# Summing the two halves of eight converted weights on TensorE instead of VectorE, with a scheduler that counts no handover within an engine

## The chip, the cores and the metric

The kernel runs on one core of a Trainium2 chip. The core has a matrix engine (TensorE, PE in the profile; PEld is its loading of weights), a vector engine (VectorE, DVE), a scalar engine (ScalarE, ACT), a general engine (GpSimd, POOL) and SyncE (SP), which here issues the DMA transfers. Each engine works through its own queue in order; semaphores order work between engines. SBUF is the working memory of 128 partitions, PSUM holds eight banks of 128 x 512 float32 that TensorE writes. The metric is the device time of one execution in microseconds, as a median of repeated runs.

## What is computed

The reference has two parts. The first is a normalised linear attention over 8 batches, 8 heads, 576 positions and a head size of 64:

```python
kv = np.einsum('bhsd,bhse->bhde', k, v)
out = np.einsum('bhsd,bhde->bhse', q, kv)
rms = np.sqrt(np.mean(out * out, axis=-1, keepdims=True) + 1e-06)
x = (out / rms * g_norm)            # then (B,H,S,D) -> (B*S, H*D): 4608 x 512
```

The second is an MLP with softplus, with w_in of 512 x 2048 and w_out of 2048 x 512:

```python
h = x @ w_in
g = np.maximum(h, 0.0) + np.log1p(np.exp(-np.abs(h)))
return (g @ w_out).astype(np.float32)
```

q, k, v and g_norm are float32, the two weight matrices float64. The kernel gets each float64 element as two 32-bit words and has to turn them into float32 itself.

## The kernel before

**Matrix products.** The large products use the F32R type of TensorE[...]. So every operand is split into three F32R parts (a high part, a remainder scaled up by 4096, and a correction), and each product is made of three passes summed in one PSUM bank.

**Stages.** Tokens are taken in 36 tiles of 128. `kv_of` (line 647) loads k and v of one batch and makes kv (matmuls of line 676, plain F32). `rows` (line 687) makes one tile of x: q is transposed (line 756 by TensorE for the first two batches, line 731 by VectorE later), multiplied by kv (line 700), squared and reduced (773, 704), its root taken on POOL (707, 708), scaled (712) and, for the first tiles, transposed by TensorE (718), split (620, 623, 626) and stored (782, 783). In a first phase, `step` (line 829) walks over blocks of 384 tokens and chunks of 128 hidden units, four chunks for the first four blocks and six for the others: `mm1` (line 843, 12 matmuls) into one of two PSUM banks of the ring "h", softplus and splitting on ScalarE and VectorE (865, 867, 854, 858), then `mm2` (line 850, 9 matmuls per step) into three banks of sums. Two later phases do the remaining hidden units in blocks of 512 tokens with fewer products by a form of fast matrix multiplication (`wide_step`, line 1008; matmuls of lines 1030 and 1100).

**Weights.** The two matrices are cut into 16 chunks each, so 32 weights of 128 x 512; weight j = 2c is chunk c of w_in and j = 2c+1 chunk c of w_out. `weight` (line 394) fetches one (512 KB, line 403) and converts it: ScalarE makes a mask (`square`, 414), VectorE makes from the high word a float32 t with the upper bits (`high1` 418, `high2` 422, `mask` 427), then its power of two p (`power`, 435), then the low word's share on the scale of p, in place (`rest`, 440), and at last `total` (444) adds t and p into w. ScalarE's `beyond` (431) records numbers out of range. `split_weight` (line 471) then makes the three parts: `high` (481 or 483, ScalarE), `low` (488 or 491, VectorE), `low_up` (494, ScalarE); for the first eight weights (c < 4) the third difference is made by TensorE in a bank of ring "h" (`less_by_pe`, 505 and 506) and read by ScalarE (509); for the others by VectorE and ScalarE (497, 501).

**What sets the order.** The order of instructions on every engine is fixed when the kernel is built, by the planner `Plan` (line 54). Each piece of work is a task with an engine, a planned duration, the tasks it comes after, a position `pos` (lower goes first among tasks that can start within 150 ns of each other) and the buffers it takes and gives back. Buffers come from rings: "m" is eight SBUF places of 128 x 512, "h" the two PSUM banks. A task's planned end is its start and duration plus the handover of its engine (line 61: 250 ns for PE, 120 for ACT and DVE, 150 for POOL, 0 for SP); a task becomes ready at the latest end of those before it (line 194). Where the planner sees a hole of 400 ns or more on PE in the opening, it puts in a dummy matmul (`warm`, line 1181), which needs a bank of ring "h" too. The lists P0 to P7 (lines 249 to 257) hold the positions: P0 those of converting and fetching the first eight weights and offsets between stages, P1 to P3 those of later weights and of the wide phases, P4 those of the 36 tiles, P5 those of kv and q, P6 those of the wide operands, P7 those of the first loads of k, v and q.

Of the kernel before, what the change touches and what calls it, by code (L numbers as in the profile page):

```python
# [8 lines left out]
F32 = mybir.dt.float32  # L9
# [9 lines left out]
P = 128  # L19
# [36 lines left out]
class Plan:  # L56
# [19 lines left out]
    def slot(self, ring):  # L76
        return Slot(ring)

    def add(self, engine, ns, run, after=(), pos=0.0, take=(), give=(), size=0, behind=None, follows=None, kind="all"):
        t = Task(engine, ns, run, [a for a in after if a is not None], pos, list(take), list(give), size)  # L80
        for s in t.give:
            s.readers += 1
        self.tasks.append(t)
        t.follows = follows
        t.behind = behind
        t.kind = kind
        return t

    def order(self):
# [5 lines left out]
        ready = {}  # L95
# [28 lines left out]
        while left:  # L124
            best = None
            for engine, tasks in ready.items():
                options = []
                for t in tasks:
                    at = max(engine_free[engine], t.ready)
                    if t.size:  # L130
                        at = max(at, dma_free - 2500)
                    for i, s in enumerate(t.take):
                        others = sum(u.ring == s.ring for u in t.take[:i])
                        if engine == "SP" and s.ring in ("m", "n"):
                            others += self.KEEP
                        if len(free[s.ring]) <= others:
                            break
                        at = max(at, sorted(free[s.ring])[sum(u.ring == s.ring for u in t.take[:i])][0])
                    else:
                        options.append((at, t))  # L140
                if not options:
                    continue
                first = min(at for at, _ in options)
                options = [(at, t) for at, t in options if at <= first + self.SOON]
                small = [o for o in options if engine == "PE" and o[1].kind != "all"]
                if small:
                    rest = [o for o in options if o[1].kind == "all"]
                    if kind != "all":
                        options = [o for o in small if o[1].kind == kind] or small
                    elif rest and len(small) < self.TOGETHER and (  # L150
                            min(o[1].pos for o in small) + self.PATIENCE > min(o[1].pos for o in rest)):
                        options = rest
                at, t = min(options, key=lambda o: (o[1].pos, o[0]))
                if engine == "PE" and self.spare and self.spare[-1].start is None:
                    ring, run, ns, _ = self.spare
                    begin = max(engine_free["PE"], self.BEGIN, min(free[ring])[0] if free[ring] else at)
                    if begin + ns <= at:
                        s = Slot(ring)
                        at, t = begin, Task("PE", ns, lambda s=s: run(s), [], None, [s], [s], 0)
                        t.kind = "all"  # L160
                        s.readers = 1
                if best is None or at < best[0]:
                    best = (at, t)
            if best is None:
                raise RuntimeError("the plan is stuck at " + str([(e, t.pos, [s.ring for s in t.take if not free[s.ring]]) for e, ts in ready.items() for t in ts][:20]))
            at, t = best
            if t in ready[t.engine]:
                ready[t.engine].remove(t)
                left -= 1
            for s in t.take:  # L170
                place = min(free[s.ring])
                free[s.ring].remove(place)
                s.place = place[1]
                if t.pos is not None:
                    coming[s.ring] = coming.get(s.ring, 0) - 1
            if t.engine == "PE":
                t.ns += self.SWITCH.get((kind, t.kind), 0)
                kind = t.kind
            t.start = at
            engine_free[t.engine] = at + t.ns  # L180
            t.end = at + t.ns + self.HANDOVER[t.engine]
            if t.size:
                dma_free = max(dma_free, at + t.ns) + t.size
                t.end = dma_free + (self.LANDING if dma_free > self.FILLED else 2000)
            for s in t.give:
                s.readers -= 1
                last_read[id(s)] = max(last_read.get(id(s), 0), t.end)
                if not s.readers:
                    free[s.ring].append((last_read[id(s)], s.place))
                    retire(s.ring)  # L190
            for u in users.get(id(t), ()):
                waiting[id(u)] -= 1
                if not waiting[id(u)]:
                    u.ready = max([a.end for a in u.after] + ([u.follows.start] if u.follows else []), default=0)
                    ready.setdefault(u.engine, []).append(u)
            done.append(t)
        return sorted(done, key=lambda t: t.start)
# [3 lines left out]
def kernel(  # L201
# [24 lines left out]
    nc = tc.nc  # L226
    B, H, S, D = q.shape
    d_model, d_ff = moe_w_in.shape
# [17 lines left out]
    STEPS = [(ph, n, p) for ph in (1, 2) for n in range(n_wide) for p in PAIRS[ph - 1][n]]  # L246
    LAST = 2

    P0 = [-45.94, -26.77, -11.8, 0.28, -29.91, -5.64, -2.86, 3.84, -103.4, -98.98, -69.3, -76.66, -68.5, -24.67, -23.22, -34.97, 8.15, -43.02, 7.47, 9.69, 7.18, 18.16, -12.1, 4.75, 1.0, 95.98, -6.45, 6.38, 7.69, 5.17]
    P4 = [-30.17, -6.08, 16.93, -33.9, -22.35, -28.91, -17.33, -7.12, -9.75, -2.59, 0.87, 2.93, -12.14, -3.26, 0.98, 3.76, 7.8, -3.0, -2.25, 7.68, 20.89, 50.27, -0.5, -0.13, 26.66, 22.67, -11.61, -5.55, 2.74, 0.64, -0.48, 1.34, 0.64, 1.68, -8.4, -1.37]  # L250
    P5 = [1.24, -5.69, -2.28, 1.58, 5.58, 0.43, 5.83, -7.56, 3.01, -2.95, 3.18, 1.42, -14.52, 0.57, -1.29, -1.34]
    P6 = [-0.39, 4.6, -0.28, -2.24, -0.01, 1.05, 1.77, -3.9, -2.15, 0.85, 1.85, -1.74, 6.34, -2.44, -0.13, 3.82, 7.89, 0.51]
    P7 = [-23.78, -17.98, -11.85, -14.93, 0.41, 1.61, 7.35, 2.7, -25.02, -6.6, -15.2, -4.48, -2.14, 0.64, 2.93, 0.97, 4.67, 5.36, 3.33, 6.57, -10.37, 2.36, -14.11, -9.89, -7.11, 12.91, -2.89, 14.55, 12.59, 9.35]
    CONVERT, FETCH, EARLY, LATER = P0[:8], P0[8:16], P0[16:27], P0[27:]
    P1 = [48.8, 48.65, 66.31, 74.64, 125.35, 131.27, -11.31, 54.26, 67.75, 469.13, 282.82, 195.86]
    P2 = [22.14, 35.93, 25.02, 37.31, 52.38, 81.67, 74.61, 116.65, 106.27, 111.35, 100.82, -152.23, 99.52, 221.41, 428.54, -173.95, 119.58, -155.43, 317.87, 212.07, -7.69]
    P3 = [3.0, 2.86, 5.84, -16.31, 1.53, 3.03, 3.55, -20.64, 3.15, 2.55, 1.38, 1.52, 1.27, 0.75, 2.42, -1.39]
    SPLIT = {p: (P1[i], P1[6 + i]) for i, p in enumerate((2, 3, 4, 5, 6, 7))}
    TAKEN = {c: (P2[c - 6], P2[4 + c]) for c in range(6, 16)}
    LEAD, APART, AHEAD, MM2, LATE, SPLIT_G = P3[0], P3[1], P3[2], P3[3:11], P3[11:14], P3[14]  # L260
# [13 lines left out]
    ident = ident_r.bitcast(F32)  # L274
# [10 lines left out]
    def space(name, words, late, dtype=F32):  # L285

        if (name, late) not in spaces:
# [13 lines left out]
                 h=2, o=2, tp=1, s0=1, s1=1, s2=1, s3=1, w=15, wh=3, u=4, u1=1, gvp=2, xl=2, ab=2)  # L301
# [9 lines left out]
    slot, add = plan.slot, plan.add  # L311
# [67 lines left out]
    wide = moe_w_in.dtype != F32  # L379
# [14 lines left out]
    def weight(j, pos, fetch_pos, behind):  # L394

        c, of_out = divmod(j, 2)
        raw, w = slot("rawb" if j % 2 and c < 8 else "raw"), slot("m")
        words = 2 if wide else 1

        def fetch():  # L400
# [6 lines left out]
        if wide:  # L407
            sq, t, p = (slot(n) for n in ("sq", "m", "m"))
# [40 lines left out]
            d2 = add("DVE", 690, high2, [d1], pos, [], [raw])  # L449
            d3 = add("DVE", 690, mask, [d2, a1], pos, [])  # L450
            over_done.append(add("ACT", 910, beyond, [d3], pos + (4 if c < 4 else 0), [], [sq]))
            d4 = add("DVE", 430, power, [d3], pos, [p, w])
            d5 = add("DVE", 690, rest, [d4], pos, [], [raw])
            ready = add("DVE", 690, total, [d3, d5], pos, [], [t, p])
        else:
            ready = add("DVE", 450, lambda: nc.vector.tensor_copy(new(w, [P, d_model]), raw.tile[:, :, 0]),
                        [f], pos, [w], [raw])
# [130 lines left out]
    def load_q(b):  # L588


        q_slots[b], q_loads[b] = slot("qa"), []
        pos = x_pos(first_tile[b] + 1) - EARLY[7] + P5[B + b]

# [555 lines left out]
    for c in range(KF):  # L1149
        for j in (2 * c, 2 * c + 1):  # L1150
            if c < OWN:
                pos = CONVERT[j] if c < 4 else LATER[c - 4] + LATER[2] * (j % 2)
                weight(j, pos, FETCH[j] if c < 4 else pos, pos - 3.5)
            else:
                fetch, pos = (x + P2[20] * (j % 2) for x in TAKEN[c])
# [61 lines left out]
```

## Time and profile before

The median of three runs is 872.99 us (872.97 to 874.07). The profiled execution took 873.68 us, and its span, from the first to the last instruction, is 871.7 us.

| engine | busy us | share of the span | instructions |
|---|---|---|---|
| PE | 858.2 | 98% | 6464 |
| PEld | 761.2 | 87% | 6464 |
| DVE | 703.9 | 81% | 992 |
| ACT | 521.4 | 60% | 979 |
| POOL | 78.3 | 9% | 79 |

Busy time is the union of an engine's instructions; an instruction's length runs from its start to its written end, and neighbours on one engine can overlap, so the step from one start to the next can be shorter than a length. The chain that ended last is followed back from the last instruction to what released it, step by step; what is not on it had slack. The granted TensorE clock is given as a share of full speed.

### The profile page before, as it was taken

What the parts mean: (1) busy time and instruction counts of PE and PEld (TensorE: products, weight loads), DVE (VectorE), ACT (ScalarE), POOL (GpSimd) and SP (SyncE); (2) the same over time, 40 slices, a digit from 0 to 9 for tenths busy, and PEclk for the clock granted to TensorE, in tenths of its full rate; (3) what the DMA queues carried; (4) which work ended last, traced back from release to release, by engine and by line L of the source; (5) the groups of instructions that cost most, each with busy time, mean ns of one, the idle gap of its engine ahead of it and who ended that gap; (6) DMA issues with size and microseconds to landing.
All of it is one profiled execution on the core that took longest, in us unless ns stands there. A gap on an engine that the chain in (4) does not pass through costs nothing.

```text
span 871.7 us, 17016 instructions
## 1 busy us (share of the span) xinstructions
PE 858.2 (98%) x6464; PEld 761.2 (87%) x6464; DVE 703.9 (81%) x992; ACT 521.4 (60%) x979; POOL 78.3 (9%) x79
## 2 busy tenths in 40 slices
PE   7899999999999999999999999999999999999998
PEld 5678888989898899988998988888899899999996
DVE  7888898988788788798988789877788766878873
ACT  5776564445353567766657556654877555566653
POOL 0351234121112300000000000000000000000000
PEclk9899999999999999999999999999999999999999
DMA  9999999898993765427544546656364653777764
GB/s 270 275 231 206 283 243 253 152 267 210 221 175 102 178 194 170 156 85 243 183 156 147 182 157 192 196 158 180 110 195 136 237 162 107 243 225 234 236 189 129
DMA packets 239634, 167.07 MB, mean 192 GB/s; under 512 B 106304, under 2 KB 198464, under 8 KB 239552
## 3 DMA queue, kind: packets, MB, share of 16 engines
q1 hardware_dynamic: 239392, 165.99, 68.2%
q8 instruction: 50, 0.82, 0.4%
q14 instruction: 32, 0.26, 0.1%
q10 hardware_dynamic: 160, 0.00, 0.0%
HBM read 112.98 MB, written 52.95 MB: 190 GB/s over the span
## 4 chain that ended last, share of the span: by engine, by line
PE 94%; DMA 2%; DVE 2%; ACT 1%; POOL 1%; issue 0%; SPq 0%; POOLq 0%; DVEq 0%; ACTq 0%
PE banks L1100 30%; PE banks L1030 28%; PE banks L850 16%; PE banks L843 15%; PE banks L700 2%; PE banks L676 2%; DMA loads<-in_k_dram 1%; DMA loads<-in_v_dram 1%; PE banks L1181 1%; PE banks L718 0%; POOL r L708 0%; DVE half L712 0%; PE banks L756 0%; SPq L403 0%; DVE units L623 0%
## 5 line engine op out<-in xcount | busy, mean ns | idle before, releaser
L1100 PE MATMUL banks<-pieces,gv 128*128 128x512 f32 x696 | 217.9, 394 | 0.0
L843 PE MATMUL banks<-units,pieces 128*128 128x384 f32 x768 | 145.8, 338 | 0.0
L850 PE MATMUL banks<-pieces,gv 128*128 128x512 f32 x576 | 145.5, 396 | 0.0
L843 PEld LDWEIGHTS banks<-units,pieces 128*128 128x128 f32 x768 | 135.1, 188 | 5.1
L1100 PEld LDWEIGHTS banks<-pieces,gv 128*128 128x128 f32 x696 | 121.2, 189 | 18.1
L1100 PE MATMUL banks<-pieces,g_False 128*128 128x512 f32 x348 | 136.4, 392 | 0.1
L1030 PEld LDWEIGHTS banks<-units,pieces 128*128 128x128 f32 x948 | 126.9, 190 | 8.3 <-ACT banks L1075 1.3
L1030 PE MATMUL banks<-units,pieces 128*128 128x256 f32 x948 | 132.5, 282 | 0.0
L850 PEld LDWEIGHTS banks<-pieces,gv 128*128 128x128 f32 x576 | 106.3, 187 | 21.0
L865 ACT ACTIVATE half<-banks 128x384 f32<-128x384 f32 x64 | 31.4, 490 | 92.3 <-PE banks L843 92.2
L1090 DVE TENSOR_TENSOR gv<-g_True,gv 128x1024 fp32r<-128x1024 f32 x48 | 58.8, 1224 | 33.9 <-ACT gv L1087 33.9
L1100 PEld LDWEIGHTS banks<-pieces,g_False 128*128 128x128 f32 x348 | 65.4, 188 | 15.3 <-DVE g_False L1093 0.6
L1079 DVE TENSOR_TENSOR g_True<-banks,g_True 128x512 f32<-128x512 f32 x48 | 33.2, 691 | 38.8 <-PE banks L1030 34.6
L708 POOL TENSOR_TENSOR r<-r,half 128x8 f32<-128x8 f32 x36 | 63.7, 1770 | 3.0
L1057 ACT ACTIVATE g_True<-banks 128x256 f32<-128x256 f32 x96 | 36.8, 383 | 39.7 <-PE banks L1030 39.2
L1093 DVE SCALAR_TENSOR_TENSOR g_False<-gv 128x1024 fp32r<-128x1024 f32 x48 | 58.7, 1224 | 1.3
L993 DVE TENSOR_TENSOR units<-loads,units 128x1024 fp32r<-128x1024 f32 x42 | 51.2, 1219 | 8.7 <-ACT units L990 8.7
L1030 PEld LDWEIGHTS banks<-units,w 128*128 128x128 f32 x396 | 52.5, 189 | 2.8
L1030 PE MATMUL banks<-units,w 128*128 128x256 f32 x396 | 54.8, 281 | 0.0
L990 ACT ACTIVATE units<-loads 128x1024 fp32r<-128x1024 f32 x42 | 44.4, 1058 | 17.0 <-PE banks L1030 11.0
L996 DVE SCALAR_TENSOR_TENSOR units<-units 128x1024 fp32r<-128x1024 f32 x42 | 51.4, 1223 | 1.6
L1087 ACT ACTIVATE gv<-g_True 128x1024 fp32r<-128x1024 f32 x48 | 51.0, 1062 | 1.5
(116 smaller groups left out, 1301.8 us busy)
## 6 DMA issues: line engine op xcount, KB each, us to landing
loads<-x SPq DMA_DIRECT2D x180, 128.0 KB, 2.8
part<-m SPq DMA_DIRECT2D x72, 256.0 KB, 2.9
m<-part SPq DMA_DIRECT2D x72, 256.0 KB, 3.4
loads<-form SPq DMA_DIRECT2D x45, 256.0 KB, 3.6
form<-loads SPq DMA_DIRECT2D x36, 256.0 KB, 2.7
raw<-in_moe_w_in_dram SPq DMA_DIRECT2D x16, 512.0 KB, 4.7
loads<-in_k_dram SPq DMA_DIRECT2D x32, 256.0 KB, 4.7
loads<-in_v_dram SPq DMA_DIRECT2D x32, 256.0 KB, 4.9
```

What stands on the lines that cost most here:

```text
L708: nc.gpsimd.tensor_tensor(out=r.tile, in0=r.tile, in1=half, op=ALU.pow)
L843: nc.tensor.matmul(hp, lhsT=w_in.tile[:, i, kd * P:(kd + 1) * P], rhs=xv.tile[:, i, kd], start=(m == 0), stop=(m == 3 * KD - 1))
L850: nc.tensor.matmul(mine[i].tile, lhsT=gv.tile[:, m, i * P:(i + 1) * P], rhs=w_out.tile[:, m], start=(c == cs[0] and m == 0), stop=(c == cs ...
L990: nc.scalar.activation(part_of(0, F32R), xl.tile if m > 1 else xl.tile[:, 0], func=AF.Copy, scale=DOWN)
L993: nc.vector.tensor_tensor(out=part_of(1, F32R), in0=xl.tile if m > 1 else xl.tile[:, 0], in1=part_of(0), op=ALU.subtract)
L996: nc.vector.scalar_tensor_tensor(out=part_of(2, F32R), in0=part_of(1), scalar=-RADIX, in1=part_of(0), op0=ALU.mult, op1=ALU.add)
L1030: nc.tensor.matmul(place(q), lhsT=w[:, m, at:at + P], rhs=dst.tile[:, m, v, kd] if u < 6 else dst.tile[:, m, kd], start=(u == 0 and not m ...
L1057: nc.scalar.activation(dst, src, func=AF.Softplus, scale=1.0 + E)
L1087: nc.scalar.activation(gvt(0, F32R), gt(), func=AF.Copy, scale=DOWN)
L1090: nc.vector.tensor_tensor(out=gvt(1, F32R), in0=gt(), in1=gvt(0), op=ALU.subtract)
L1093: nc.vector.scalar_tensor_tensor(out=gt(F32R), in0=gvt(1), scalar=-RADIX, in1=gvt(0), op0=ALU.mult, op1=ALU.add)
L1100: nc.tensor.matmul(mine[i].tile, lhsT=(gvt(m, F32R) if m < 2 else gt(F32R))[:, c, i * P:(i + 1) * P], rhs=outs[c].tile[:, m], start=fresh ...
```

## The change

The diff has three parts. In `weight`, for c < 4, w is no longer an SBUF buffer of ring "m" but a bank of ring "h", and the sum of t and p is made by two F32 matmuls with the identity that accumulate in it; the readers of w (`high` and `low`) then read PSUM. In the planner, a task that comes after another of the same engine becomes ready without that engine's handover. And the positions P0 to P7 have other values.

```diff
-                    u.ready = max([a.end for a in u.after] + ([u.follows.start] if u.follows else []), default=0)
+                    u.ready = max([a.end - (a.engine == u.engine) * self.HANDOVER[a.engine] for a in u.after] + ([u.follows.start] if u.follows else []), default=0)
...
-    P0 = [-45.94, -26.77, -11.8, 0.28, -29.91, -5.64, -2.86, 3.84, -103.4, -98.98, -69.3, -76.66, -68.5, -24.67, -23.22, -34.97, 8.15, -43.02, 7.47, 9.69, 7.18, 18.16, -12.1, 4.75, 1.0, 95.98, -6.45, 6.38, 7.69, 5.17]
-    P4 = [-30.17, -6.08, 16.93, -33.9, -22.35, -28.91, -17.33, -7.12, -9.75, -2.59, 0.87, 2.93, -12.14, -3.26, 0.98, 3.76, 7.8, -3.0, -2.25, 7.68, 20.89, 50.27, -0.5, -0.13, 26.66, 22.67, -11.61, -5.55, 2.74, 0.64, -0.48, 1.34, 0.64, 1.68, -8.4, -1.37]
+    P0 = [-30.37, -15.76, -45.84, 0.42, -5.68, -5.18, -0.38, 1.26, -133.49, -126.15, -85.66, -65.85, -81.89, -31.8, -11.39, -16.9, 10.42, -55.23, 19.13, 12.85, 4.83, 3.56, -5.48, 4.19, -0.26, 207.14, -17.96, 4.89, 7.52, 8.87]
+    P4 = [-40.55, 6.27, -7.55, 3.46, -14.1, -8.87, -27.21, -0.38, -26.83, 4.82, 5.31, -0.3, -37.28, -19.2, 3.24, -1.14, 15.19, -1.69, -1.03, 18.1, 53.19, 68.55, -8.34, -8.03, 89.66, 28.98, -1.75, -13.32, 1.36, -32.25, 0.74, 2.82, 0.24, 28.59, 0.14, -4.09]
...
-        raw, w = slot("rawb" if j % 2 and c < 8 else "raw"), slot("m")
+        raw, w = slot("rawb" if j % 2 and c < 8 else "raw"), slot("h" if wide and c < 4 else "m")
...
-            d4 = add("DVE", 430, power, [d3], pos, [p, w])
+            d4 = add("DVE", 430, power, [d3], pos, [p, w] if c >= 4 else [p])
             d5 = add("DVE", 690, rest, [d4], pos, [], [raw])
-            ready = add("DVE", 690, total, [d3, d5], pos, [], [t, p])
+            if c < 4:
+                bank = w
+
+                def total_by_pe():
+                    y = new(bank, [P, d_model])
+                    nc.tensor.matmul(y, lhsT=ident, rhs=t.tile.bitcast(F32), start=True, stop=False)
+                    nc.tensor.matmul(y, lhsT=ident, rhs=p.tile.bitcast(F32), start=False, stop=True)
+
+                ready = add("PE", 1870, total_by_pe, [d3, d5], pos, [bank], [t, p])
+            else:
+                ready = add("DVE", 690, total, [d3, d5], pos, [], [t, p])
```

The lists P1, P2, P3, P5, P6 and P7 are replaced in the same way.

More of the change, by code (lines that the diff above doesn't have):

```diff
@@ L247 @@
     LAST = 2
-    P0 = [-45.94, -26.77, -11.8, 0.28, -29.91, -5.64, -2.86, 3.84, -103.4, -98.98, -69.3, -76.66, -68.5, -24.67, -23.22, -34.97, 8.15, -43.02, 7.47, 9.69, 7.18, 18.16, -12.1, 4.75, 1.0, 95.98, -6.45, 6.38, 7.69, 5.17]
-    P4 = [-30.17, -6.08, 16.93, -33.9, -22.35, -28.91, -17.33, -7.12, -9.75, -2.59, 0.87, 2.93, -12.14, -3.26, 0.98, 3.76, 7.8, -3.0, -2.25, 7.68, 20.89, 50.27, -0.5, -0.13, 26.66, 22.67, -11.61, -5.55, 2.74, 0.64, -0.48, 1.34, 0.64, 1.68, -8.4, -1.37]
-    P5 = [1.24, -5.69, -2.28, 1.58, 5.58, 0.43, 5.83, -7.56, 3.01, -2.95, 3.18, 1.42, -14.52, 0.57, -1.29, -1.34]
@@ L252 @@
-    P6 = [-0.39, 4.6, -0.28, -2.24, -0.01, 1.05, 1.77, -3.9, -2.15, 0.85, 1.85, -1.74, 6.34, -2.44, -0.13, 3.82, 7.89, 0.51]
-    P7 = [-23.78, -17.98, -11.85, -14.93, 0.41, 1.61, 7.35, 2.7, -25.02, -6.6, -15.2, -4.48, -2.14, 0.64, 2.93, 0.97, 4.67, 5.36, 3.33, 6.57, -10.37, 2.36, -14.11, -9.89, -7.11, 12.91, -2.89, 14.55, 12.59, 9.35]
+    P0 = [-30.37, -15.76, -45.84, 0.42, -5.68, -5.18, -0.38, 1.26, -133.49, -126.15, -85.66, -65.85, -81.89, -31.8, -11.39, -16.9, 10.42, -55.23, 19.13, 12.85, 4.83, 3.56, -5.48, 4.19, -0.26, 207.14, -17.96, 4.89, 7.52, 8.87]
@@ new lines @@
+    P4 = [-40.55, 6.27, -7.55, 3.46, -14.1, -8.87, -27.21, -0.38, -26.83, 4.82, 5.31, -0.3, -37.28, -19.2, 3.24, -1.14, 15.19, -1.69, -1.03, 18.1, 53.19, 68.55, -8.34, -8.03, 89.66, 28.98, -1.75, -13.32, 1.36, -32.25, 0.74, 2.82, 0.24, 28.59, 0.14, -4.09]
+    P5 = [-10.83, -23.81, -4.58, 19.0, -3.07, -1.88, -1.53, -3.13, 33.52, 23.45, -7.31, -3.18, -21.75, 2.88, -1.17, -3.09]
+    P6 = [4.67, 4.37, 5.18, 8.18, -7.04, 11.44, 10.27, 3.43, 2.96, -18.16, 5.57, 13.01, -0.03, 12.26, 12.34, 8.53, 11.92, 11.21]
@@ L254 @@
+    P7 = [-27.32, -56.98, -0.28, -16.68, 11.77, 22.77, 17.31, 3.39, -30.48, 24.34, -17.2, -13.8, -11.19, -14.83, -8.17, 11.34, 13.75, -7.15, -10.02, 17.79, -6.46, -25.59, -1.64, -43.37, -21.06, 6.17, 3.9, 2.13, 23.78, 27.71]
     CONVERT, FETCH, EARLY, LATER = P0[:8], P0[8:16], P0[16:27], P0[27:]
-    P1 = [48.8, 48.65, 66.31, 74.64, 125.35, 131.27, -11.31, 54.26, 67.75, 469.13, 282.82, 195.86]
-    P2 = [22.14, 35.93, 25.02, 37.31, 52.38, 81.67, 74.61, 116.65, 106.27, 111.35, 100.82, -152.23, 99.52, 221.41, 428.54, -173.95, 119.58, -155.43, 317.87, 212.07, -7.69]
@@ L257 @@
-    P3 = [3.0, 2.86, 5.84, -16.31, 1.53, 3.03, 3.55, -20.64, 3.15, 2.55, 1.38, 1.52, 1.27, 0.75, 2.42, -1.39]
+    P1 = [51.23, 54.04, 55.59, 78.23, 120.42, 131.22, -16.2, 28.19, 71.97, 305.26, 156.52, 141.86]
+    P2 = [37.79, 28.21, 20.86, 42.97, 47.24, 82.45, 76.6, 115.29, 109.05, 103.03, 223.34, -176.44, 86.19, 314.98, 377.41, -364.8, 145.34, -291.7, 251.05, 225.04, -8.78]
+    P3 = [4.39, 1.82, 6.23, -27.38, -0.84, 4.92, 4.85, -26.84, 4.47, 4.73, 0.44, 2.49, -3.29, -9.27, 0.27, 0.9]
     SPLIT = {p: (P1[i], P1[6 + i]) for i, p in enumerate((2, 3, 4, 5, 6, 7))}
```

## The prediction

> **What bounds the kernel now.** I read the page first: share of each engine, then the chain that ended last.
>
> ```profile
> span 871.7 us, 17016 instructions
> PE 858.2 (98%) x6464; PEld 761.2 (87%) x6464; DVE 703.9 (81%) x992; ACT 521.4 (60%) x979; POOL 78.3 (9%) x79
> PE 94%; DMA 2%; DVE 2%; ACT 1%; POOL 1%; issue 0%; SPq 0%; POOLq 0%; DVEq 0%; ACTq 0%
> ```
>
> TensorE (PE) carries the chain, and PE is what the change gives more work. But "busy" hides filler: the planner puts a dummy matmul (`warm`, line 1181) into planned holes of PE. So next I cut the first 80 us into stretches, for all engines (columns: length, then PE, PEld, DVE, ACT, POOL busy with counts, clock, DMA share, GB/s) ...
>
> ```profile
> 0.00:8.00 8.00, 4.96 (x13) 3.62 (x13) 4.62 (x13) 3.08 (x5) 0.93 (x7) 1.00 0.78 237
> 8.00:20.00 12.00, 10.84 (x107) 7.76 (x108) 9.87 (x17) 8.18 (x16) 0.00 (x0) 0.86 1.19 297
> 20.00:30.00 10.00, 7.89 (x114) 6.00 (x109) 8.49 (x15) 6.36 (x14) 4.17 (x4) 0.79 1.07 272
> 30.00:40.00 10.00, 9.10 (x126) 6.76 (x125) 7.93 (x13) 8.41 (x17) 2.71 (x4) 0.87 1.10 279
> 40.00:47.00 7.00, 6.16 (x117) 4.77 (x116) 6.43 (x12) 5.53 (x12) 2.89 (x3) 1.00 1.01 227
> 47.00:60.00 13.00, 12.10 (x160) 10.42 (x162) 11.33 (x20) 9.55 (x20) 5.59 (x7) 1.00 1.02 222
> 60.00:80.00 20.00, 19.44 (x262) 15.85 (x262) 17.42 (x32) 12.62 (x26) 7.85 (x7) 1.00 0.93 235
> ```
>
> ... and for line 1181 alone (PE, PEld, clock, DMA, GB/s).
>
> ```profile
> 8.00:20.00 12.00, 5.79 (x16) 3.08 (x16) 0.86 1.19 297
> 20.00:30.00 10.00, 2.81 (x6) 1.46 (x6) 0.79 1.07 272
> 30.00:40.00 10.00, 3.34 (x8) 1.71 (x9) 0.87 1.10 279
> 40.00:47.00 7.00, 2.06 (x8) 1.05 (x6) 1.00 1.01 227
> ```
>
> Between 8 and 47 us PE has 14.0 us of filler (5.79+2.81+3.34+2.06) and 5.0 us idle (1.16+2.11+0.90+0.84): 19.0 us of room. From 47 to 60 it is 0.49 filler and 0.90 idle, from 60 to 80 0.50 and 0.56; from 80 to 850 us PE is busy throughout, and 4.3 us of its last 22 are idle. So the kernel is two stages: an opening that ends near 60 us, bound by what feeds PE, and a PE-bound rest. In the opening VectorE (DVE) is busy 44.1 of the 52 us from 8 to 60 (85%), and the main DMA queue is full too; this is its line for the first 70 us:
>
> ```profile
> q1 hardware_dynamic: 36690, 17.77, 101.1%
> ```
>
> The chain through the opening (start us, length us, what) shows that DVE's place in it is real, the removed `total` (L444) included:
>
> ```profile
> 47.01 2.11 PE banks L843 x12
> 49.12 0.44 PE banks L718 x4
> ...
> 54.64 1.15 PE banks L676 x32
> ...
> 56.55 0.69 DVE half L712
> 57.24 0.60 DVE m L444
> 57.84 0.47 DVE gv L854
> 58.31 0.61 DVE r L704
> ```
>
> The first mm1 starts at 47.0 us; the chain before 26 us goes mostly through k and v loads of 4.8 to 6.5 us.
>
> **What the Trainium skill says.** (1) "FP8 and Floating Point Precision", TensorE Precision Notes: true FP32 takes four passes. The trace agrees in kind: each F32 kv product of line 676 stands as two matmul records (eight calls, x16), and an F32 transpose of 128 columns takes 0.44/4 = 0.11 us, twice 128 cycles at the 2.4 GHz that "TensorE: Matmul & The Clock Gate" gives; two records at half rate are four passes. (2) "PSUM — Partial Sum Buffer", on bank collisions: two engines must not touch one bank at once, so the sum, its ScalarE (ACT) and DVE readers go one after the other and hold the bank. (3) "Perfetto Trace Analysis", Optimizing Scalar/DVE Operations, makes PSUM access dearer for DVE (about 125 against 60 ns) and cheaper for ACT; here the DVE subtraction of line 623 takes 0.688 us from a bank and 0.681 from SBUF, so I charge nothing.
>
> **The change, part by part.**
>
> *Removed: eight `total` on DVE.* Each is 0.69 us long, but the next one starts 0.60 us later (57.16 to 57.76). As it needs `rest`, it also starts 0.73 us after `rest` (7.18 to 7.91) where independent neighbours keep 0.60: 0.13 more. Relief 8 x 0.73 = 5.8 us of DVE, 4.8 if something else pays the 0.13. They stand at 7.9, 12.2, 18.3, 22.6, 33.3, 43.6, 57.2 and 69.7 us.
>
> *Added: eight sums on PE*, two F32 identity matmuls over 512 columns. No such row exists before. From the transpose: 512/128 x 0.11 = 0.44 us a record, two records a matmul, two matmuls: 1.76 us. Lower bound: each record at the rate of an F32R matmul, nine in 2.10 us, 4 x 0.233 = 0.93 us. Upper: at kv's rate, 32 in 1.15 us with two side by side, 0.072 us for 64 columns, 8 x 4 x 0.072 = 2.3 us. I take 1.76 us, 14.1 in all (7.5 to 18.4); at the opening's clock of 0.79 to 0.87 some sums take 2.0 to 2.2 us. They hide in the 19.0 us of room: the six before 47 us need 10.6 to 13. Without that cover they cost their full length, as after 60 us. In PE's order, kv products, transposes and `rows` stand behind a sum, and SP's queue behind kv: SP already waited 3.1 us for line 676 to free load buffers, so a sum ahead of a kv batch can delay loads by up to 1.76 us.
>
> *Latency and banks.* From `rest` to a usable weight: 1.76 us and two handovers in place of 0.73, about +1.2 us. Hidden for weights 0 to 5, which wait for the first mm1 at 47 us; not for 6 and 7. The sum sits in one of two h banks, which mm1, the filler and the existing PE step of the same weight use, from its start until the split's `high` (0.72) and `low` (0.75) have read it: some 3.3 us x 8 = 26 us in two banks over 60 us. The first mm1s hold a bank 2.6 us each from 47 us on. There is room early, little after 47. One SBUF m buffer fewer per weight is needed; no wait of the page is on it: nothing gained.
>
> *Scheduler: no handover within an engine.* It changes planned times, not instructions. Planned 690+120 ns for a dependent DVE pair, real 0.73; now 690. The plan may then set dependents back to back at 0.13 us each: perhaps 10 more such pairs in the opening, +1.3 us of DVE, or none. On PE, 250 ns between dependent mm1 was false: they run end to end in the trace. I take 0, -1 to +1.5.
>
> *Moved: all positions in P0 to P7.* These reorder every engine and the SP queue; DMA bytes are the same. Block 0's third tile moves ahead of most weights (its position falls from -9.8 to -42), block 1's first tile behind them (-37.4 to -11.7), the eighth weight up (3.84 to 1.26). That brings first steps forward and takes less attention work ahead. After 80 us a new order can only lose, or save switches of PE (2.10 us against 2.28 for a preceded mm1): -2 to +4; I take 0.
>
> *Sum.* The advance of the first steps: the sums removed before 47 us, 6 x 0.73 = 4.4, times DVE's 85% share = 3.7, and the seventh's 0.60, which lies on the chain: 4.3 us earlier. Against it: the seventh sum finds 1.39 us of room between 47 and 60, so 0.4 stays; the eighth comes in the PE-bound stage, 1.76: 2.2 us. PE's denser opening also gains a little clock: from 8 to 40 us a granted clock of 0.79 to 0.87 costs some 5 us of full clock, most of it under filler and holes; I take 0.4. Net -4.3 + 2.2 - 0.4 = -2.5 us. The profiled execution took 873.7 us (span 871.7, 2.0 around it), 0.7 above the median 873.0 of the runs. So 871.2 on its own scale, **870.5 us** as a median.
>
> **Rivals.**
>
> *A. The loads set the opening (no change).* For: the queue at 101%, the chain up to 26 us through loads. Against: from 33 to 62 us the chain holds no load. Then relief gains only what the exposed sums cost: 873 us, 871.3 to 874.7.
>
> *B. Exposed sums (slower).* Place: PE after 47 us. If the new order starts the first steps earlier, with less PE work done ahead, or if weights 5 to 7 stay late, three or four sums fall where PE has no hole: 3.5 x 1.76 = 6.2, less an advance of 3: +3.2, 876.2 us; up to 878 with 0.2 to 0.4 us more per sum. It decides once exposed sums times 1.76 exceed the advance: at 2.4 sums for 4.3 us. For: two of eight totals now end after 57 us. Against: relief moves conversions ahead.
>
> *C. A better order altogether.* All eight sums hidden, 5.8 us of relief realised and a few PE switches saved: 865 to 867 us. Against: PE then needs nearly every hole of the opening, which dependent pieces of 0.4 to 1.2 us do not allow.
>
> *D. The new order makes PE wait after 80 us*, where it now never does: one stall of 3 us gives 876, slower also.
>
> The edit does what it says: the sums are there in any case.
>
> **Chances.** This kernel's measurement tells about 0.2% (1.7 us) from no change. Forecast 0.36 (867.5 to 871.2), C 0.08, A 0.20, B 0.27, D 0.09. Faster 0.44, same 0.20, slower 0.36. The range 866 to 877 leaves out the far half of C and the far ends of B and D; the forecast's own is 867.5 to 871.2.
>
> **What would show it.** DVE busy falls by about 5.5 us, PE's F32 sums measure about 1.76 us for four records, fillers fall from 52 to some 20 to 30; the first mm1 starts near 43 us; at most two sums after the last hole of PE; PE idle after 80 us below 1 us until the tail. I am wrong if three or more sums stand behind that point (B), if k and v loads land no earlier and mm1 starts at 47 us (A), or if waits of PE appear after 80 us (D).

## The result: 0.45% slower

The changed kernel takes 877.25 us in the median (876.45 to 877.36), against 872.98 us (872.66 to 874.07) for the kernel before on the same chip: a ratio of 1.0045 (95% interval 1.0027 to 1.0062), or +3.9 us. The forecast was 870.5 us, with a range up to 877.

Its profiled execution took 877.36 us. First the page: span, share of each engine, chain that ended last.

```profile
span 875.6 us, 17010 instructions
...
PE 860.1 (98%) x6463; PEld 759.6 (87%) x6463; DVE 699.0 (80%) x984; ACT 520.5 (59%) x979; POOL 75.6 (9%) x79
...
PE 94%; DMA 2%; DVE 2%; ACT 1%; POOL 0%; issue 0%; SPq 0%; DVEq 0%; POOLq 0%; ACTq 0%
```

DVE lost 4.9 us of busy time, as intended, and PE still carries 94% of the chain. PE's busy time rose by only 1.9 us although some 14 us of sums came in. Two views show why. The stretches of the opening, all engines, in the columns of the prediction:

```profile
8.00:20.00 12.00, 11.14 (x105) 7.05 (x102) 8.12 (x15) 7.76 (x16) 0.00 (x0) 1.00 1.16 294
20.00:30.00 10.00, 7.07 (x106) 4.06 (x102) 8.27 (x14) 6.13 (x13) 4.04 (x4) 1.00 1.19 236
30.00:40.00 10.00, 8.16 (x116) 5.79 (x118) 7.22 (x13) 7.51 (x15) 1.90 (x2) 1.00 1.08 285
40.00:47.00 7.00, 6.58 (x103) 5.01 (x98) 5.68 (x10) 5.44 (x11) 3.57 (x4) 1.00 1.11 270
47.00:60.00 13.00, 12.22 (x125) 9.34 (x123) 10.97 (x19) 10.26 (x21) 4.66 (x5) 1.00 1.05 193
60.00:80.00 20.00, 19.90 (x281) 16.28 (x280) 16.80 (x30) 11.45 (x24) 3.96 (x4) 1.00 0.90 201
```

And the filler alone, now at line 1191 (PE, PEld, clock, DMA, GB/s):

```profile
8.00:20.00 12.00, 3.20 (x6) 1.23 (x6) 1.00 1.16 294
20.00:30.00 10.00, 0.00 (x0) 0.00 (x0) 1.00 1.19 236
30.00:40.00 10.00, 1.42 (x4) 0.68 (x4) 1.00 1.08 285
40.00:47.00 7.00, 0.00 (x0) 0.00 (x0) 1.00 1.11 270
```

From 8 to 60 us DVE is now busy 40.3 us where it was 44.1: most of the freed time became idle time. From 8 to 47 us the filler fell from 14.0 to 4.6 us, and PE's idle time rose from 5.0 to 6.1. Over the whole run the filler is 8.8 us (19 pieces) against 19.9 (52), and idle time is 15.5 us against 13.5. So PE's ledger is: +13.8 us of sums (eight of 1.72), -11.1 of filler, +2.0 idle, and -0.8 for all other work, which gives the +3.9 of the span. The sums took the filler's place and more; nothing was left over for the real work to come forward.

The chain that ended last (start, length, what) now has sums on it:

```profile
22.07 7.95 DMA loads<-in_k_dram
30.16 0.69 PE banks L686 x16
...
43.47 0.86 PE banks L459 x2
44.33 0.86 PE banks L460 x2
45.19 0.44 PE banks L766 x4
45.62 2.11 PE banks L853 x12
...
50.85 1.05 PE banks L459 x2
51.91 0.86 PE banks L460 x2
...
67.66 0.86 PE banks L459 x2
68.52 0.86 PE banks L460 x2
```

Lines 459 and 460 are the two matmuls of a sum: 0.86 us each at full clock, so 1.72 us a sum (the first sum, at 9.30 us, takes longer). The first mm1 (line 853) starts at 45.4 us instead of 47.0, but the second and third start at 55.1 and 60.0 where they started at 52.1 and 56.4. The chain waits 8 us for a k load at 22 us, and from 32.6 to 40.0 us it runs through VectorE for 6.8 us. A v load ends PE's longest wait of the opening, as in the kernel before, where that wait was 1.9 us:

```profile
29.20 0.69 PE L686 MATMUL banks<-loads 128*64 128x64 f32 x16 [2.81 <-DMA loads<-in_v_dram]
```

This is the first kv product of the second batch, in PE's timeline; in the kernel before the same product (line 676) ran at 26.27 us. After 80 us PE has one wait, of 1.1 us, until its tail, where the kernel before had none. The rest of the loss is there by then: from 80 us on PE still has 790.52 us of work to do, against 787.75 before. These 2.8 us and the wait make up the 3.9 of the span.

### The profile page after: what moved, and what is told of

Its sections match the earlier page's. It is cut to its first block, busy times and chain, and to the rows that moved or that the text cites. A ratio compares the mean times of both kernels' runs of the same rounds, so it can differ in the third digit from the quotient of the medians.

```text
span 875.6 us, 17010 instructions
## 1 busy us (share of the span) xinstructions
PE 860.1 (98%) x6463; PEld 759.6 (87%) x6463; DVE 699.0 (80%) x984; ACT 520.5 (59%) x979; POOL 75.6 (9%) x79
## 4 chain that ended last, share of the span: by engine, by line
PE 94%; DMA 2%; DVE 2%; ACT 1%; POOL 0%; issue 0%; SPq 0%; DVEq 0%; POOLq 0%; ACTq 0%
PE banks L1110 30%; PE banks L1040 27%; PE banks L860 15%; PE banks L853 15%; PE banks L710 2%; PE banks L686 2%; DMA loads<-in_k_dram 1%; DMA early<-in_q_dram 1%; PE banks L728 1%; PE banks L459 0%; PE banks L460 0%; DVE half L722 0%; POOL r L718 0%; ACT half L783 0%; PE banks L766 0%
## 5 line engine op out<-in xcount | busy, mean ns | idle before, releaser
L1040 PE MATMUL banks<-units,pieces 128*128 128x256 f32 x1032 | 142.7, 282 | 0.0
L1040 PEld LDWEIGHTS banks<-units,pieces 128*128 128x128 f32 x1032 | 136.8, 190 | 6.5
L853 PEld LDWEIGHTS banks<-units,pieces 128*128 128x128 f32 x768 | 135.3, 188 | 4.7 <-DVE m L498 0.2
L1067 ACT ACTIVATE g_True<-g_True 128x512 f32<-128x512 f32 x48 | 30.3, 632 | 41.7 <-DVE g_True L1089 40.8
L905 ACT ACTIVATE m<-banks 128x512 f32<-128x512 f32 x72 | 42.1, 596 | 16.1 <-PE banks L1110 11.5
```

What stands on the lines that cost most here:

```text
L853: nc.tensor.matmul(hp, lhsT=w_in.tile[:, i, kd * P:(kd + 1) * P], rhs=xv.tile[:, i, kd], start=(m == 0), stop=(m == 3 * KD - 1))
L1040: nc.tensor.matmul(place(q), lhsT=w[:, m, at:at + P], rhs=dst.tile[:, m, v, kd] if u < 6 else dst.tile[:, m, kd], start=(u == 0 and not m ...
L1067: nc.scalar.activation(dst, src, func=AF.Softplus, scale=1.0 + E)
```

## The experiments

In the expectations letters stand for theories; M and O are explained in the first of them. The two that stayed to the end are: the late sums lie bare on PE, and taking them off PE gives the time back (X); the order of the opening and its loads hold the time, whatever engine makes the sum (Y). Ratios are to runs of the kernel before on the same chip.

**One part at a time, planned anew.** Four kernels each keep a part of the change and let the planner write the order: the sums alone (f_sums), the new positions alone (f_pos), both with the old handover rule (f_sums_pos), and the rule and positions with `total` back on VectorE (f_hand_pos).

```diff
 f_sums:      sum by PE;   old positions;  u.ready = max([a.end for a in u.after] ...
 f_pos:       total on DVE; new positions; u.ready = max([a.end for a in u.after] ...
 f_sums_pos:  sum by PE;   new positions;  u.ready = max([a.end for a in u.after] ...
 f_hand_pos:  total on DVE; new positions; u.ready = max([a.end - (a.engine == u.engine) * ...
```

> The kernel before with the eight sums moved to TensorE, old positions, old handover rule. Theory M (the sums' TensorE time finds no cover, and the DVE time they free was not what held the opening): 875 to 880 us. Theory O (the new positions cost the time, the sums are covered): 870 to 873.5 us. In both the sums measure 1.72 us each, as after.

> The kernel before with the new positions P0 to P7 alone: the sum stays on DVE, old handover rule. Theory M: 870 to 874 us, since no TensorE work is added. Theory O: 876 us or more.

> The changed kernel with the old handover rule. Both theories: if the handover rule does little, 876 to 878.5 us as after; if the new positions only fit the new rule, above 879 us.

> The changed kernel with the sums back on DVE (new positions and new handover rule kept). Theory M: the 13.9 us of TensorE sums are gone and the 5 us of DVE are back, so 870 to 874.5 us. Theory O: 876 to 879 us.

Measured: 1.0318 (1.0300 to 1.0336), 1.0241 (1.0226 to 1.0257), 1.0221 (1.0206 to 1.0237) and 1.0235 (1.0219 to 1.0251). All are 19 to 28 us slower than before. For f_sums and f_hand_pos this is far outside what either theory gave; f_pos and f_sums_pos fall only into ranges that had no upper end ("876 us or more", "above 879 us"). The positions seem to be fitted to the durations and the rule with which they were planned: each of the four mixtures gives a poor order, with waits of PE between 100 and 390 us that neither kernel has. So these runs price no part. The new rule with the old positions was not run, so it has no price of its own. From here on the order of instructions is held fixed.

**The sum's length, in the order after.** g_half_sum makes each sum with one matmul, g_double_sum makes it twice.

```diff
 g_half_sum
-nc.tensor.matmul(y, lhsT=ident, rhs=t..., start=True, stop=False)
-nc.tensor.matmul(y, lhsT=ident, rhs=p..., start=False, stop=True)
+nc.tensor.matmul(y, lhsT=ident, rhs=t..., start=True, stop=True)
 g_double_sum
+nc.tensor.matmul(y, lhsT=ident, rhs=t..., start=True, stop=False)
+nc.tensor.matmul(y, lhsT=ident, rhs=p..., start=False, stop=True)
```

> The changed kernel in its own order on every engine, but each sum is one matmul instead of two (the power of two and the rest in p are left out of eight weights), 0.86 us less of TensorE each, 6.9 us in all. Theory M with all sums bare: 870.4 us. Theory M with only the last two or three bare: 874.5 to 875.6. If all sums are covered and only the order matters: 877 us.

> The changed kernel in its own order, each sum made twice (four matmuls), 1.72 us more of TensorE each, 13.8 us in all. All bare: 891 us. Two or three bare: 880.5 to 882.5. All covered: 877 us.

Measured: 1.0035 (1.0023 to 1.0046) and 1.0159 (1.0139 to 1.0180). Doubling adds 13.8 us of PE work and costs 10 us over the kernel after: longer sums are mostly bare. Halving takes 6.9 us off PE and returns about 0.9 us, which is within the noise (the intervals overlap), and its stretches show a second change:

```profile
20.00:30.00 10.00, 6.76 (x121) 4.58 (x119) 8.24 (x14) 6.13 (x13) 3.82 (x4) 0.89 1.23 244
30.00:40.00 10.00, 8.79 (x79) 6.33 (x76) 5.68 (x9) 5.93 (x13) 1.29 (x2) 0.60 1.05 285
```

The granted clock fell to 0.60 from 30 to 40 us, where the kernel after has 1.00, so this execution has two causes in it and cannot stand for the price of a sum.

**VectorE's relief, taken by itself, in the order before.** g_double_total makes `total` of the first eight weights twice (DVE's busy time rises by 4.5 us); g_more_loads adds eight copies of 256 KB, one behind each of their fetches.

```diff
 g_double_total, in total()
+if c < 4:
+    nc.vector.tensor_tensor(out=w.tile, in0=t.tile.bitcast(F32), in1=p.tile.bitcast(F32), op=ALU.add)
 g_more_loads, in fetch()
+if c < 4:
+    nc.sync.dma_start(out=dram.tile([P, d_model], U32, ...), in_=moe_w_out.bitcast(U32)[...])
```

> The kernel before in its own order, with the DVE total of the first eight weights made twice, about 0.6 us more of DVE each, 4.8 us in all. If DVE holds the opening, as predicted (85% of it on the path), 876 to 878 us. If DVE has slack there: 873 to 874 us, and the predicted relief of 4.3 us does not exist.

> The kernel before in its own order, with a copy of 256 KB within DRAM after the fetch of each of the first eight weights: 2.1 MB more for the DMA queue in the opening, 8 us at its rate of 255 GB/s for reading alone. If the loads hold the opening: 878 to 884 us. If they have slack: 873 to 875 us.

Measured: 1.0003 (0.9991 to 1.0015) and 1.0049 (1.0030 to 1.0068). Eight more operations of the removed kind cost the kernel nothing that can be seen, while 2.1 MB more on the main queue cost 4.3 us (the bytes, or the eight more issues of 0.5 to 0.6 us each in SyncE's queue: the two are not separated). The forecast's step had a slope of about 0.85 us per us of DVE; here it is at most 0.29 (0.0015 x 873 / 4.5). One caveat: the granted clock of g_double_total is 1.00 from 20 to 40 us, where the kernel before has 0.79 and 0.87, and may have paid for a part.

More work need not mirror less work, so the last run of the study took work away. l_no_rest leaves out `rest` of the first eight weights, an operation as long as `total`, and changes nothing else.

```diff
 def rest():
+    if c < 4:
+        return
     pf = p.tile.bitcast(F32)
```

> The kernel before in its own order of instructions, with the VectorE operation `rest` of the first eight weights left out (the share of the low words is then not multiplied in; all else is computed). It is as long as the removed `total` (0.69 us), so this gives VectorE the relief of the change, 8 x 0.60 to 0.73 = 4.8 to 5.8 us, and shortens each weight's chain by the same, with nothing added on TensorE and no new position. If the relief is worth its share of the opening (the forecast's step), it is 4.3 us faster: ratio 0.9951. If VectorE's relief is worth next to nothing in an opening that is held by loads and by the order (theory Y), the ratio lies within 0.998 to 1.001, DVE's busy time is 5 us lower, and the first mm1 starts less than 1 us earlier than 46.9 us.

Measured: 1.0004 (0.9997 to 1.0012). This is the relief of the change with none of its costs, and in this order it is worth nothing. From its page, and then PE's waits of the first 47 us (total, times, longest) in l_no_rest:

```profile
PE 859.7 (98%) x6464; PEld 762.5 (87%) x6464; DVE 698.5 (80%) x984; ACT 522.3 (60%) x979; POOL 78.5 (9%) x79
```

```profile
PE banks L678 <- DMA loads<-in_v_dram: 3.5, 2, 1.9
...
PE banks L758 <- DVE units L625: 0.6, 1, 0.6
```

and the same view of the kernel before, which was there to be read before the forecast:

```profile
PE banks L676 <- DMA loads<-in_v_dram: 3.2, 2, 1.9
PE banks L1181 <- DVE ident_r L1141: 1.6, 1, 1.6
PE banks L700 <- ACT half L773: 0.6, 1, 0.6
PE banks L756 <- DVE units L623: 0.6, 1, 0.6
```

DVE did fall by 5.4 us, and what ends PE's waits is what it was. The longest are ended by v loads. What VectorE ended, after the identity at the very start, is 0.6 us and one more of 0.2. One limit of this run: the filler stays in PE's queue, so in this order a relief could have shortened only the idle part of the room, 5.0 us from 8 to 47. That is more than the 4.3 us forecast, but only just; what relief is worth in an order planned without that filler was not run. The profiled execution of l_no_rest took 877.77 us, 3 above its median, and its first mm1 starts at 49.2 us, later than the 46.9 of the kernel before; so its times within the opening are not used.

**The sums on PE, in the order before.** h_old_six makes the first six totals as PE sums in the position that `total` had, and drops four fillers for each; no position is new.

```diff
 def total():
+    sums_made.append(j)
+    if len(sums_made) <= 6:
+        w.tile = banks[:, 6]
+        spared[0] += 4                      # warm() returns at once so many times
+        nc.tensor.matmul(w.tile, lhsT=ident, rhs=t..., start=True, stop=False)
+        nc.tensor.matmul(w.tile, lhsT=ident, rhs=p..., start=False, stop=True)
+        return
```

> The kernel before in its own order, but the first six totals are made by the two TensorE matmuls (in a PSUM bank that is free until the first mm2), at the place in TensorE's order that the plan gave to the total; four fillers are left out for each. No new positions. As predicted blind (the six hide, the freed DVE time brings the first steps forward): 869.3 us. Theory X (the freed DVE time is worth nothing, the early sums are covered, the late ones are bare): 872.5 to 874.5 us. If even the early sums are not covered: 878 us or more.

Measured: 1.0027 (1.0018 to 1.0035), +2.4 us where my steps gave -3.7. PE's timeline of it:

```profile
17.85 0.69 PE L684 MATMUL banks<-loads 128*64 128x64 f32 x16
19.27 1.02 PE L449 MATMUL banks<-m,ident_r 128*128 128x512 f32 x2
20.13 1.02 PE L450 MATMUL banks<-m,ident_r 128*128 128x512 f32 x2
21.08 0.69 PE L684 MATMUL banks<-loads 128*64 128x64 f32 x16
...
28.12 0.69 PE L684 MATMUL banks<-loads 128*64 128x64 f32 x16
```

The same kv products in the kernel before:

```profile
16.53 0.69 PE L676 MATMUL banks<-loads 128*64 128x64 f32 x16
19.10 0.69 PE L676 MATMUL banks<-loads 128*64 128x64 f32 x16 [0.29 <-DMA loads<-in_k_dram]
26.27 1.12 PE L676 MATMUL banks<-loads 128*64 128x64 f32 x16 [1.27 <-DMA loads<-in_v_dram]
```

PE takes its work in order. A sum stands directly ahead of the fourth kv product, which starts 2.0 us later, and the second batch's first product 1.9 us later. These products free the buffers into which the next k and v loads go. SyncE issues the next k load at 18.58 us instead of 17.25. As relief alone is worth nothing (l_no_rest), the 2.4 us (1.6 to 3.1) are the price of six early sums, all of which lie ahead of the point where I had put them down as hidden. Which part of it comes through the delayed loads, and which through the later weights or the 24 fillers left out, is argued from the lines, not isolated. The clock took no time here: it is 1.00 in every stretch of h_old_six.

**Early or late sums, in the order after.** The first five sums, all before 37.5 us, or the last three, at 43.3, 50.8 and 67.5 us, are made longer or shorter.

```diff
 h_late_half / h_late_double / h_early_double: in total_by_pe
+sums_made.append(j)
+late = len(sums_made) > 5
 h_late_half:    one matmul if late, else two
 h_late_double:  four matmuls if late, else two
 h_early_double: two matmuls if late, else four
```

> The changed kernel in its own order; only the last three sums (43.5, 50.9 and 67.7 us) are one matmul instead of two, 2.6 us less of TensorE in all, where the clock is full and no filler stands (p is left out of three weights). Theory X (late sums bare): 874.7 us. Theory Y (all sums covered, only the new order costs): 877.3 us.

> The changed kernel in its own order; the last three sums are made twice, 5.2 us more of TensorE. Theory X: 882.4 us. Theory Y: 877.3 to 879 us.

> The changed kernel in its own order; the first five sums are made twice, 8.6 us more of TensorE. Doubling all eight cost 11.3 us. Theory X: the rest of it, 883.4 us, so the early sums have used up their cover and the next microsecond there is not free. Theory Y: 886 us or more.

Measured: 1.0024 (1.0014 to 1.0035), 1.0096 (1.0078 to 1.0114), 1.0086 (1.0070 to 1.0101). Over the kernel after, 5.2 us more in three late sums cost 4.5 us (0.87 us per us), and 8.6 us more in five early ones cost 3.6 (0.42). Each of these differences is uncertain by some 2 us, so that the late slope is the steeper one is likely, not certain. Longer late sums are nearly bare, but early ones are not free either. Halving the late ones takes 2.6 us away and gives about 1.8 back; its interval overlaps that of the kernel after, so this is unclear; taken at its word, it stands nearer to X, which has all 2.6 given back, than to Y.

**The late sums off PE, in the order after.** If late sums are bare, one DVE operation of 0.6 to 0.7 us in their place should return most of their 5.2 us. i_late_dve does that for the last three, i_all_dve for all eight, writing the same bank.

```diff
 def total_by_pe():
+    sums_made.append(j)
+    if len(sums_made) > 5:          # i_all_dve: > 0
+        nc.vector.tensor_tensor(out=y, in0=t.tile.bitcast(F32), in1=p.tile.bitcast(F32), op=ALU.add)
+        return
```

> The changed kernel in its own order and with its positions; the last three sums (43.5, 50.9, 67.7 us) are made by one DVE addition into the same PSUM bank, at the place in DVE's order where the plan had the sum on TensorE; the first five stay on TensorE. Theory X (late sums bare, DVE with slack): 5.2 us of TensorE gone at a slope of 0.7 to 0.9, so a ratio of 0.999 to 1.001 to the kernel before. Theory Y (the new order costs, not the sums): 1.003 to 1.005.

> The same with all eight sums on DVE, so that only order, positions and handover rule differ from the kernel before, and fewer fillers. Theory X: the early five gain nothing more, a ratio of 0.999 to 1.002 (a little more if TensorE's clock drops where sums kept it busy). If early sums cost too: 0.995 to 0.998. Theory Y: 1.003 to 1.005.

Measured: 1.0039 (1.0025 to 1.0053) and 1.0058 (1.0045 to 1.0072). Neither gives the time back that X promised. i_late_dve from 47 to 80 us:

```profile
47.00:60.00 13.00, 10.12 (x110) 7.65 (x110) 11.50 (x20) 10.05 (x21) 4.32 (x4) 1.00 1.12 209
60.00:80.00 20.00, 18.43 (x276) 15.40 (x275) 17.18 (x31) 11.87 (x26) 3.96 (x4) 1.00 0.90 201
```

and PE's waits from 40 to 110 us:

```profile
PE banks L715 <- ACT w L778: 1.4, 1, 1.4
PE banks L733 <- ACT pieces L498: 1.3, 1, 1.3
PE banks L715 <- ACT half L788: 1.1, 1, 1.1
PE banks L865 <- DVE gv L869: 0.6, 1, 0.6
PE banks L733 <- DVE units L638: 0.5, 1, 0.5
```

PE was idle 0.88 us from 47 to 80 in the kernel after (0.78 + 0.10) and is idle 4.45 here (2.88 + 1.57): the 3.4 us of the two sums that lay there turned into holes. By PE's timeline ScalarE ended 3.0 us of these 4.45 and VectorE 1.3. (The wait of 1.1 us in the list stands at 84 us and is the one that the kernel after has too.) The second mm1 starts only 0.5 us earlier than in the kernel after, although the first starts 1.9 earlier.

```profile
68.50 0.63 PE L733 MATMUL banks<-ident_r,half 128*128 128x128 f32 x4 [1.26 <-ACT pieces L498]
```

A part of these holes is the new work on VectorE itself. In the largest hole after 60 us, this one, the moved sum (67.06 us) stands directly ahead of the VectorE operation that makes `half` (67.68 to 68.36), which the transposes of this line read. So X as it was put fell: moving the late sums to VectorE, in this order, returns about 0.5 us, which is within the noise. It does not follow that a late sum only fills a wait that is there anyway; what leaving it out altogether is worth, h_late_half leaves unclear. i_all_dve carries a second cause, as g_half_sum did: from 8 to 20 us its clock is 0.57.

```profile
8.00:20.00 12.00, 8.98 (x64) 5.66 (x61) 9.98 (x17) 8.10 (x16) 0.00 (x0) 0.57 1.17 295
```

**The loads, in the order after.** j_loads_first moves a k load, a kv product and the second batch's first loads ahead of fetches and of the first sum. It put a load ahead of the reader of its buffer, so its time (1.0101) says nothing; j_loads_first2 also moves that reader. k_more_loads_after adds the copies of g_more_loads to the kernel after.

```diff
 j_loads_first2: in the finished order
+ahead(("load", 0, 1, 0), first_q)
+ahead(("kv", 0, 1), at["sum", 0])
+ahead(("kv", 0, 3), at["fetch", 4])
+ahead(("load", 1, 0, 0), at["fetch", 4])
+ahead(("load", 1, 0, 1), at["fetch", 4])
```

> The changed kernel with four moves in its own order and nothing else: the second k load of the first batch is issued ahead of the first q load, the second kv product of that batch stands ahead of the first sum on TensorE, and the first k and v loads of the second batch are issued ahead of the fifth weight. Theory Y, with the loads of k and v named as the place (in every kernel with the new positions the second kv product starts at 12.4 to 13.0 us and the second batch's kv at 27.9 to 29.3, against 10.6 and 26.3 before, whether or not the sums are on TensorE): second kv near 11, second batch near 26.5 us, and 2 of the 3.9 us come back, a ratio near 1.002. If the loss lies elsewhere in the order: these starts move, the time stays at 1.004 to 1.005.

> The four moves of the run before, with one mended: the first loads of the second batch now stand behind the fourth kv product of the first batch, whose buffer one of them takes. If the place of these loads is where the time went: second batch's kv near 27 us or earlier and a ratio near 1.002. If not: 1.004 to 1.006, or worse where the moves delay something else.

> The changed kernel in its own order with the 2.1 MB of extra copies that cost the kernel before 4.3 us. If loads hold the opening of the changed kernel too: 4 to 6 us more than it, a ratio of 1.009 to 1.0115. If TensorE's sums or DVE hold it: 1.0045 to 1.006.

Measured: 1.0063 (1.0050 to 1.0076) for j_loads_first2 and 1.0074 (1.0060 to 1.0088) for k_more_loads_after. The second batch's first product came forward from 29.20 to 27.80 us, and the run did not become shorter (1.6 us longer, within the noise): earlier k and v loads alone, at the expense of the fetches, do not mend the order. The added copies cost about 2.5 us here and 4.3 in the kernel before, so more work in the load queue is not free in either, and in the kernel after no dearer than before; the second cost is uncertain by some 2 us. Like more `total`, more loads do not say what fewer would give. Of Y it is shown only that changing the late sums' engine in the finished order does not give the time back; that order and loads hold it is not shown. Which moved position carries how much of it stays open. No version of these runs beats the kernel before.

## Why the prediction was wrong, point by point

- **The failed step is "The advance of the first steps: ... 4.3 us earlier".** It took VectorE's busy share of the opening, 85%, as the share of its time that lies on the path. l_no_rest took as much VectorE time away as the change does and gained nothing (1.0004), and g_double_total doubled `total` at no cost that can be seen. The chain of the kernel before could have said so: from 8 to 47 us it runs through VectorE for only 5.2 of the 39 us (some of its pieces are shown here) and through k and v loads for some 14, and the only `total` (L444) on it in the first 80 us is the one at 57.24:

```profile
9.58 0.75 DVE m L488
10.33 0.61 DVE m L427
...
11.42 0.70 DVE m L440
...
37.00 0.70 DVE units L623
...
41.48 0.70 DVE half L712
```

The piece that I showed was true of one place. That without it other work arrives at nearly the same time is inferred from l_no_rest, not traced.
- **A second step failed: "They hide in the 19.0 us of room".** Of that room, from 8 to 47 us, filler and idle time gave 14.0 and 5.0 us, and 8.3 us of the 19.0 came out (10.7 remain: 4.6 filler, 6.1 idle). But hiding was not free. The risk was named, a sum ahead of a kv batch delaying loads, and priced at nothing. h_old_six shows the delay (1.3 to 2.0 us for each of three products) and 2.4 us at the end.
- **The sum with the two terms put right:** -2.5 + 4.3 (no advance) + 2.4 (early sums) = +4.2 us, where +3.9 was measured. The agreement is closer than the terms deserve: they were measured in the order before, and the share of the new order, which all the moved positions make, is not separated.
- **The price of a sum was right:** 1.76 us estimated from a transpose and the Trainium skill's four passes ("FP8 and Floating Point Precision", TensorE Precision Notes), 1.72 measured. Whether the two late sums cost the 2.2 us put down stays open: the slope of 0.87 for longer ones would make it near 3.0, and i_late_dve got only about 0.5 back for three.
- **The counts:** DVE down 4.9 us (5.5 expected); 19 fillers (20 to 30 expected); the first mm1 at 45.4 us (43 expected).
- **After 80 us** I expected no cost and less than 1 us of idle time; one wait of 1.1 us came. So rival D is there in small, with 1.1 of its 3 us. Rival B came near the right time (876.2) by luck, as its way was another: it had three or four sums behind 47 us, and there are two. Rival A was right that relief alone is worth nothing, and wrong that only the exposed sums would then cost anything; its own sign, a first mm1 at 47 us, did not come. Rival C asked for a better order; none of the runs shows one.

## What to carry to other kernels

The busy share of an engine that is not the bound is no price for its relief (here 85%, and nothing gained): read which engine ends the waits of the one that is (VectorE ended about 0.8 us of PE's waits in the first 47 us, the very first wait aside, and k and v loads 3.5), how much of the chain the engine has, or leave one of its operations out and look. Filler in holes is room only for work that nothing waits behind: in an in-order queue a sum put into a hole delays what follows it, here the products that free load buffers. A list of positions fitted to one set of durations could not be tested part by part by planning anew (19 to 28 us lost each time); hold the order and change one duration.

## What the runs showed of the hardware

TensorE's clock differed between these kernels, and this clouds some comparisons. In the profiled execution of the kernel after the granted clock is given as 1.00 in every stretch (although a filler at 8.71 us takes 0.80 us and one at 18.07 takes 0.39), where the kernel before had 0.79 to 0.87 from 8 to 40 us. With half of each sum gone it was 0.60 from 30 to 40 us, and with no sums on PE 0.57 from 8 to 20. One execution proves little here: h_late_double starts with the same instructions as the kernel after and had 0.86 from 8 to 20. But for i_all_dve all five executions agree: their mean granted clock is 0.984 to 0.988, that of the kernel after 0.996 to 0.999.

The Trainium skill ("TensorE: Matmul & The Clock Gate", The HAM clock gate) describes a clock that falls to half rate after an idle window of about 3.4 us of PE and rises again after a busy one. The 0.57 agrees in kind, with 3.0 us of the 12 idle, but no single wait there is longer than 2.20 us, and the kernel after was idle 2.9 of the 10 us from 20 to 30 at 1.00; so these runs do not show the rule.

What the lost clock costs can only be estimated. Among the 27 to 31 executions of the kernel before that ran beside the g and h runs, the time is 0.3 to 0.4 us longer for each 0.001 of mean clock lost. The mean clock of i_all_dve lies 0.010 below that of the kernel before beside it, so some 3 to 4 us of its 5.1 may go with the clock, if the clock is the cause and not the effect of waits. In that case the new order with all sums on VectorE costs only 1 to 2 us by itself, and i_all_dve says little against X. The full clock of the kernel after did not make it faster than the kernel before.
